# FoX attention and spectral mixing on one core: the first half of the mode weights loaded one row per partition, w_ch and the first mode products moved, f loaded on the Activation queue

## The chip, the cores and the metric

The kernel runs on one core of a Trainium2 chip. The metric is the device time of one execution in microseconds. All inputs are float32 in HBM, and the output is float32 in HBM.

## The reference, cut to what matters

Two layers are computed, one after the other. The first is causal attention with a decay that comes from forget gates f; the second mixes 64 frequency modes of the sequence with one complex matrix each, and adds a channel product.

```python
# B, H, S, Dh = 8, 8, 576, 64;  D = H * Dh = 512;  64 modes
scores = q @ k^T / sqrt(Dh) + cumsum(log f)[i] - cumsum(log f)[j], causal
x = softmax(scores) @ v                        # -> x[b, s, d], d over (h, Dh)
X  = rfft(x, axis=s)[:, :64]                   # Xr, Xi
Yr = einsum('bmd,mde->bme', Xr, w_r) - einsum('bmd,mde->bme', Xi, w_i)
Yi = einsum('bmd,mde->bme', Xr, w_i) + einsum('bmd,mde->bme', Xi, w_r)
u  = x + irfft(Yr + 1j * Yi, n=576)
out = u + relu(u @ w_ch)
```

The weights w_r and w_i are [64, 512, 512] each: 134 MB in float32 together. q, k and v are 28 MB together, w_ch is 1 MB, the output 9.4 MB.

## The kernel before, in words

**Weights.** The 64 modes' weights are cut into NT = 64 tiles of 2 MB, each loaded once into a ring of NRING = 9 buffers (`wpool`) and cast to bf16 on the way. `emit_w_load(n)` (L91) issues two DMAs for a tile, one for w_r and one for w_i, through `pool_dma`, which is GpSimd's queue in program order; the profile puts all of these under L89. Tiles 0 to 31 (n < NTH) hold rows of the first half of d, four modes a tile. Tiles 32 to 63 hold the second half of d, two modes a tile with two neighbouring rows of d in each partition. In the kernel before, tiles 0 to 31 also take two neighbouring rows of d per partition, 4 KB of HBM in one piece, with w_r on the even partitions and w_i on the odd ones (L95 to L101).

**Mode products.** `emit_modes(n)` (L118) multiplies one tile: for each of its modes and each of four blocks of e there are two (first half) or four (second half) matmuls that add up in one PSUM tile `A` of pool `psM`, which has one buffer during attention; then VectorE copies or adds `A` into `Yacc` (L155, L157) or into `YT` (L161). This frees the tile's ring buffer, and `next_w()` (L640) issues the load of the next one.

**Attention.** 32 steps s, two for each pair `pr` of (d block, batch pair). A step has the score products (L505), the exponentials on ScalarE (L512), the products with v (L550) and transposes. `emit_loads` (L215) brings k, q and v of a pair on GpSimd's queue, three buffers deep; only f (L247) and the v of the first two pairs (L226) go on SP's queue. At even steps `emit_dft` (L574) takes a finished pair to 64 modes: matmuls with the basis `bas` (L593), then, for the first half of d, copies to a tile `T` (L603, L604), four matmuls with the selection matrices `sel` that spread rows over even and odd partitions (L618), and one copy to `XT` (L629). For the last block of d there is only a strided copy (L607) and a strided negation (L611).

**Order.** The step loop (L649) loads weight tiles ahead up to the ninth in the first steps; from step 9 on it calls `emit_modes` at the end of each step, 32 tiles in 24 steps. w_ch is issued at step 10, behind the loads of the tenth tile (number 9, issued in step 9) and of a pair's k, q and v. The order that instructions take on each engine is made by the framework from the order of the program's calls, and so differs from it in places; GpSimd's DMAs keep the program's order, and in the trace no more than eight of them are outstanding at a time.

**After attention.** Tiles 32 to 63 are multiplied; between the first of them lie the products of x with w_ch (`emit_xw`, L712). After the last tile come the inverse transform, the sum and the stores (L824 to L894).

Of the kernel before, what the change touches and what calls it, by code (L numbers as in the profile page):

```python
# [8 lines left out]
F32 = mybir.dt.float32  # L9
BF16 = mybir.dt.bfloat16  # L10
# [5 lines left out]
def _strided(ap: bass.AP, free_dims, offset_elems: int = 0) -> bass.AP:  # L16
    new_ap = [list(ap.ap[0])] + [list(x) for x in free_dims]
    return bass.AP(tensor=ap.tensor, offset=ap.offset + offset_elems, ap=new_ap)
# [3 lines left out]
def kernel(  # L22
# [11 lines left out]
    nc = tc.nc  # L34
# [11 lines left out]
    MG = 4  # L46
# [20 lines left out]

    ident_bf = const.tile([128, 128], BF16, name="ident_bf")
    wch = const.tile([128, NDC, D], BF16, name="wch")
    bas = const.tile([128, NSB + 1, 2, NM], BF16, name="bas")  # L70
    sel = [const.tile([128, 130], BF16, name=f"sel{r}") for r in range(2)]
    BI = const.tile([128, SP], BF16, name="BI")

    wtiles = {}
# [16 lines left out]
    def emit_w_load(n):  # L91
        dc, g = tile_of(n)
        if n < NTH:
            wb = wpool.tile([128, MG, 2 * D], BF16, tag="wb", name="wb")
            for t, src in enumerate((moe_w_r, moe_w_i)):  # L95
                pool_dma(
                    wb[t:128:2, :, :],
                    src[
                        g * MG : (g + 1) * MG, dc * 128 : (dc + 1) * 128, :
                    ].rearrange("m (p r) e -> p m (r e)", r=2),  # L100
                )  # L101
        else:
            wb = wpool.tile([128, 2, M2, 2 * D], BF16, tag="wb", name="wb")
            parts = 2 if n == NT - 1 else 1
            for h in range(parts):
                ms = slice(h * M2 // parts, (h + 1) * M2 // parts)
                for t, src in enumerate((moe_w_r, moe_w_i)):
                    pool_dma(
                        wb[:, t, ms, :],
                        src[g * M2 : (g + 1) * M2, D // 2 : D, :][ms].rearrange(  # L110
                            "m (p r) e -> p m (r e)", r=2
                        ),
                    )
        wtiles[n] = wb
# [3 lines left out]
    def emit_modes(n):  # L118
# [8 lines left out]
        else:  # L127
            A = late["psM"].tile([128, NDC, nm, 2 * B], F32, tag="A", name="A")
        if n < NTH:
            terms = [  # L130
                (lambda mi, es, r=r: wb[:, mi, r * D + es : r * D + es + 128],
                 lambda m, r=r: XT3s[dc][:, r, :, m])
                for r in (0, 1)
            ]
        else:
            terms = [
                (lambda mi, es, t=t, r=r: wb[:, t, mi, r * D + es : r * D + es + 128],
                 lambda m, c0=c0, r=r: XT3s[2 + r][:, m, c0 : c0 + 2 * B])
                for t, c0 in ((0, B), (1, 0))
                for r in (0, 1)  # L140
            ]
        for mi in range(nm):
            m = g * nm + mi
            for eb in range(NDC):
                for i, (w_of, x_of) in enumerate(terms):
                    nc.tensor.matmul(  # L146
                        A[:, eb, mi, :],
                        lhsT=w_of(mi, eb * 128),
                        rhs=x_of(m),
                        start=(i == 0),  # L150
                        stop=(i == len(terms) - 1),
                    )
# [19 lines left out]
    with ExitStack() as actx:  # L172
# [4 lines left out]
        vap = actx.enter_context(tc.tile_pool(name="vap", bufs=2))  # L177
        epl = actx.enter_context(tc.tile_pool(name="epl", bufs=1))
        nrm = actx.enter_context(tc.tile_pool(name="nrm", bufs=4))
        tpl = actx.enter_context(tc.tile_pool(name="tpl", bufs=1))  # L180
        ssb = actx.enter_context(tc.tile_pool(name="ssb", bufs=1))
        late["psM"] = actx.enter_context(
            tc.tile_pool(name="psM", bufs=1, space=bass.MemoryType.PSUM)
# [60 lines left out]
        ident_f = scratch(128, 128)  # L244
        ftf = scratch(128, S)
        ft = ftf[:BH, :]
        nc.sync.dma_start(ft[:], f.rearrange("b h s -> (b h) s"))  # L247
        emit_loads(0)
        nc.gpsimd.memset(trimask[:, :], 1.0)
        nc.gpsimd.affine_select(  # L250
# [33 lines left out]
            nc.gpsimd.iota(m_i[:], pattern=[[1, NM]], base=0, channel_multiplier=0)  # L284
        )
        nc.vector.tensor_copy(ident_f[:, :], ident_bf[:, :])
        for r, t in enumerate(sel):
            nc.vector.memset(t[:, :], 0.0)
            nc.vector.tensor_copy(
                _strided(t[:, 1:2], [[2, 64]]), _strided(ident_bf[:, r : r + 1], [[2, 64]])  # L290
            )
        for t in VTs:
            nc.vector.memset(t[:, :, S:SP], 0.0)
        for t in KTs:
# [75 lines left out]
        def emit_basis():  # L370
# [1 line left out]
            RND = 12582912.0  # L372
            TURN = 2.0 * math.pi / S * (1.0 - 2.0e-7)
            NB1 = NSB + 1
            s_f = scratch(128, NB1)
            nc.vector.tensor_copy(s_f[:], s_i[:])
            m_f = scratch(128, NM)
            nc.vector.tensor_copy(m_f[:], m_i[:])
            ang = wide[:, 0 : 2 * NB1 * NM].rearrange(
                "p (a b c) -> p a b c", a=2, b=NB1  # L380
# [25 lines left out]
            nc.scalar.activation(Zt[:, :, :, 1], ang[:, 1, :, :], ACT.Sin, scale=-TURN)  # L406
            nc.vector.memset(Zt[64:128, 4, :, :], 0.0)
            nc.vector.memset(Zt[0:64, 5, :, :], 0.0)
            nc.vector.tensor_copy(
                bas[:, :, :, :], Zt[:, :, :, :].rearrange("p s m t -> p s t m")  # L410
            )
            coef = ssb.tile([128, 1], F32, name="coef")
            nc.vector.memset(coef[:], 2.0 / S)
            nc.vector.memset(coef[0:2, :], 1.0 / S)
# [159 lines left out]
        def emit_dft(pr):  # L574
            dc, bp, _ = steps[2 * pr]
            if dc == 2:
                return
            forms = [(dc, dc * 128, 1)] if dc < 2 else [(2, 256, 2), (3, 257, 2)]
            if dc < 2:
                if bp == 0:  # L580
                    XT3s[dc] = xtpool.tile(
                        [128, 2, 2 * B, NM], BF16, tag="XT3", name=f"XT{dc}"
                    )
                T = tpl.tile([128, 3, 2, NM], BF16, tag="T", name="T")
            for b in (2 * bp, 2 * bp + 1):
                for c, d0, st in forms:
                    if b == 0 and dc == 3:
                        XT3s[c] = xtpool.tile(
                            [128, NM, 3 * B], BF16, tag="XT3", name=f"XT{c}"
                        )  # L590
                    px = psT.tile([128, 2, NM], F32, tag="tr", name="px")
                    for sb in range(NSB):
                        nc.tensor.matmul(  # L593
                            px[:, :, :],
                            lhsT=_strided(
                                x_all[:, bp, xi(b, sb), d0 : d0 + 1], [[st, 128]]
                            ),
                            rhs=bas[:, sb if sb < 4 else 4 + b % 2, :, :],
                            start=(sb == 0),
                            stop=(sb == NSB - 1),  # L600
                        )
                    if dc < 2:
                        nc.vector.tensor_copy(T[:, 1:3, b % 2, :], px[:, :, :])  # L603
                        nc.scalar.mul(T[:, 0, b % 2, :], px[:, 1, :], -1.0)  # L604
                        continue
                    XT3 = XT3s[c]
                    nc.vector.tensor_copy(  # L607
                        _strided(XT3[:, 0, B + b : B + b + 1], [[B, 2], [3 * B, NM]]),
                        px[:, :, :],
                    )  # L610
                    nc.scalar.mul(  # L611
                        _strided(XT3[:, 0, b : b + 1], [[3 * B, NM]]), px[:, 1, :], -1.0
                    )
            if dc < 2:
                px2 = psT.tile([128, 2, 4 * NM], F32, tag="tr", name="px2")
                for r in (0, 1):
                    for t in (0, 1):
                        nc.tensor.matmul(  # L618
                            px2[:, r, :],
                            lhsT=sel[r][:, 1 - t : 129 - t],  # L620
                            rhs=T[:, 1 - t : 3 - t, :, :].rearrange(
                                "p c b m -> p (c b m)"
                            ),
                            start=(t == 0),
                            stop=(t == 1),
                            skip_group_check=True,
                        )
                XT = XT3s[dc]
                nc.vector.tensor_copy(  # L629
                    _strided(  # L630
                        XT[:, 0, 2 * bp, 0:1], [[2 * B * NM, 2], [B * NM, 2], [1, 2 * NM]]
                    ),
                    px2[:, :, :].rearrange("p r (c n) -> p r c n", c=2),
                )

        NS = len(steps)
        nload = 2
# [2 lines left out]
        def next_w():  # L640
            nonlocal nload
            if nload < NDC * NG:
                emit_w_load(nload)
                nload += 1
# [4 lines left out]
        for s in range(NS + 1):  # L649
# [2 lines left out]
                emit_loads(pr + STG - 1)  # L652
            if s < 10 and nload < min(NRING, 3 + 3 * s // 4):
                next_w()
            if s == 10:
                pool_dma(wch[:], moe_w_ch.rearrange("(eb p) e -> p eb e", p=128))
            if pr + 1 < NPR:
                emit_transposes(pr + 1, ("kq", "v")[h])
# [4 lines left out]
            if s < NS:  # L663
                emit_scores(s, 1)
                emit_scores(s, 2)
            if s >= 1:
                emit_av(s - 1, [3, 4])
            if s < NS:
# [2 lines left out]
            if s >= 1:  # L671
                vaugs.pop(s - 1)
                if h == 0:
                    emit_dft(pr - 1)
            if s > B:
                while nmode < (s - B) * NTH // (NS - B):
                    emit_modes(nmode)
                    nmode += 1
                    next_w()

    with ExitStack() as bctx:
        bsb = bctx.enter_context(tc.tile_pool(name="bsb", bufs=1))
# [255 lines left out]
```

## Time and profile before

| | us |
|---|---|
| median of 4 runs | 448.65 |
| lowest and highest | 447.41, 451.7 |
| the profiled execution | 447.73 |
| its span | 446.0 |
| TensorE busy | 335.0 |
| VectorE busy | 240.8 |
| ScalarE busy | 198.1 |
| GpSimd busy | 138.8 |

The profiled execution's own time is 1.73 us above its span. The mean granted TensorE clock is 0.806. The DMA engines moved 97.27 MB as counted at the destination, where most weights are bf16; HBM was read for 163.73 MB. A packet of a first-half weight tile is 4096 B in HBM and 2048 B in SBUF; one of w_ch is 2048 B and 1024 B.

A GB/s in a view counts bytes at the destination, so a stretch with only weights shows half of what is read. POOL is GpSimd, and a row of POOL at L89 is the issuing of one DMA, not its transfer. DMA share can be above 1, since packets of one engine overlap.

### The profile page before, as it was taken

What the parts mean: (1) busy time and instruction counts of PE and PEld (TensorE: products, weight loads), DVE (VectorE), ACT (ScalarE), POOL (GpSimd) and SP (SyncE); (2) the same over time, 40 slices, a digit from 0 to 9 for tenths busy, and PEclk for the clock granted to TensorE, in tenths of its full rate; (3) what the DMA queues carried; (4) which work ended last, traced back from release to release, by engine and by line L of the source; (5) the groups of instructions that cost most, each with busy time, mean ns of one, the idle gap of its engine ahead of it and who ended that gap; (6) DMA issues with size and microseconds to landing.
All of it is one profiled execution on the core that took longest, in us unless ns stands there. A gap on an engine that the chain in (4) does not pass through costs nothing.

```text
span 446.0 us, 11215 instructions
## 1 busy us (share of the span) xinstructions
PE 335.0 (75%) x4823; PEld 231.2 (52%) x4823; DVE 240.8 (54%) x614; ACT 198.1 (44%) x296; POOL 138.8 (31%) x194
## 2 busy tenths in 40 slices
PE   2388888999897987877877886999973247437993
PEld 1255656687665665656655665566662124323431
DVE  6768988868466555654566675233320002103893
ACT  3378877777343536436547281434320002102442
POOL 6333330532332323323323231132333232200661
PEclk9999999999766656658769595999985559756998
DMA  8999999699999999999999999999999999991697
GB/s 204 210 236 238 237 237 236 104 234 211 237 237 210 237 214 233 236 214 233 237 214 233 211 211 211 211 211 211 211 211 212 211 211 211 212 190 26 223 377 282
DMA packets 50048, 97.27 MB, mean 218 GB/s; under 512 B 3376, under 2 KB 12080, under 8 KB 50000
## 3 DMA queue, kind: packets, MB, share of 16 engines
q0 software_dynamic: 46096, 85.34, 98.1%
q1 hardware_dynamic: 3824, 11.09, 6.9%
q8 instruction: 38, 0.62, 0.5%
q10 hardware_dynamic: 80, 0.13, 0.1%
q14 instruction: 10, 0.08, 0.0%
HBM read 163.73 MB, written 9.44 MB: 388 GB/s over the span
## 4 chain that ended last, share of the span: by engine, by line
PE 40%; DMA 24%; ACT 13%; DVE 11%; issue 4%; SPq 1%; POOL 1%; DVEq 0%; ACTq 0%; POOLq 0%
DMA wb<-in_moe_w_i_dram 20%; ACT E L512 9%; PE pav L550 7%; PE A L146 6%; PE ps L505 6%; PE tp L453 6%; PE pxw L729 5%; DMA stv<-in_v_dram 3%; DVE QTs L468 2%; ACT KT L466 2%; PE vp L477 2%; PE px L593 2%; PE ptr L718 2%; DVE E L527 1%; DVE XT L607 1%
## 5 line engine op out<-in xcount | busy, mean ns | idle before, releaser
L512 ACT ACTIVATE E<-ps 128x1024 bf16<-128x1024 f32 (+1 forms) x128 | 101.7, 851 | 21.4 <-PE ps L505 14.9
L146 PE MATMUL A<-XT,wb 128*128 128x16 bf16 x2048 | 71.7, 182 | 47.3 <-DMA wb<-in_moe_w_i_dram 26.1
L146 PEld LDWEIGHTS <-wb 128*128 128x128 bf16 x2048 | 64.4, 101 | 58.5 <-DMA wb<-in_moe_w_i_dram 28.3
L89 POOL DMA_DIRECT2D wb<-in_moe_w_r_dram x65 | 43.7, 672 | 150.8 <-PE A L146 57.1
L505 PE MATMUL ps<-QTs,KT 64*128 64x64 bf16 (+4 forms) x384 | 57.0, 317 | 18.2 <-ACT E L512 17.5
L89 POOL DMA_DIRECT2D wb<-in_moe_w_i_dram x65 | 43.3, 667 | 66.7 <-DMA wb<-in_moe_w_r_dram 32.3
L550 PE MATMUL pav<-va,E 128*128 128x65 bf16 (+1 forms) x1088 | 54.5, 209 | 3.2 <-DVE va L483 1.5
L550 PEld LDWEIGHTS <-E 128*128 128x128 bf16 (+1 forms) x1088 | 45.1, 114 | 17.7 <-issue 10.0
L527 DVE TENSOR_TENSOR E<-E,trimask 128x256 bf16<-128x256 bf16 (+2 forms) x128 | 36.9, 302 | 20.4 <-ACT E L512 20.2
L161 DVE TENSOR_TENSOR YT<-A,Yacc 128x128 bf16<-128x128 f32 x24 | 8.9, 369 | 68.5 <-PE A L146 68.5
L470 ACT COPY VT<-tp 128x640 bf16<-128x640 bf16 (+1 forms) x32 | 23.3, 760 | 31.6 <-PE tp L453 31.5
L505 PEld LDWEIGHTS <-KT 64*128 64x128 bf16 x384 | 18.7, 98 | 29.9 <-issue 21.2
L466 ACT COPY KT<-tp 128x640 bf16<-128x640 bf16 (+1 forms) x32 | 21.9, 742 | 26.4 <-PE tp L453 26.4
L736 ACT CAST XW<-pxw 128x512 bf16<-128x512 f32 x36 | 20.3, 587 | 29.9 <-PE pxw L729 29.9
L729 PE MATMUL pxw<-wch,yy 128*128 128x512 bf16 x144 | 33.6, 383 | 0.0
L468 DVE COPY QTs<-tp 128x640 bf16<-128x640 bf16 (+1 forms) x32 | 23.2, 767 | 13.4 <-PE tp L453 13.2
L572 DVE TENSOR_TENSOR x_all<-pav,rcp 128x384 bf16<-128x384 f32 x64 | 29.0, 454 | 0.8
L748 ACT CAST yy<-pyw 128x512 bf16<-128x512 f32 x8 | 4.7, 586 | 51.9 <-PE pyw L741 51.9
L877 POOL TENSOR_TENSOR uo<-uo 128x1024 f32<-128x1024 f32 x7 | 16.5, 2359 | 29.9 <-DVE uo L870 26.2
L441 DVE TENSOR_TENSOR vb<-stv,wdec 128x1152 bf16<-128x1152 f32 x16 | 21.6, 1351 | 3.9 <-PE tp L453 3.9
L561 DVE RECIPROCAL rcp<-pav 128x6 f32<-128x6 f32 x64 | 12.1, 189 | 21.3 <-PE pav L550 20.5
L729 PEld LDWEIGHTS <-yy 128*128 128x128 bf16 x144 | 13.4, 99 | 16.7 <-DVE yy L723 4.4
(115 smaller groups left out, 460.7 us busy)
## 6 DMA issues: line engine op xcount, KB each, us to landing
wb<-in_moe_w_r_dram POOLq DMA_DIRECT2D x63, 512.0 KB, 16.2
wb<-in_moe_w_i_dram POOLq DMA_DIRECT2D x63, 512.0 KB, 16.5
out_dram<-uo SPq DMA_DIRECT2D x16, 512.0 KB, 3.7
stv<-in_v_dram POOLq DMA_DIRECT2D x14, 576.0 KB, 15.2
stk<-in_k_dram POOLq DMA_DIRECT2D x16, 288.0 KB, 15.2
stq<-in_q_dram POOLq DMA_DIRECT2D x16, 288.0 KB, 15.2
stv<-in_v_dram SPq DMA_DIRECT2D x2, 576.0 KB, 7.3
out_dram<-uo SPq DMA_DIRECT2D x7, 128.0 KB, 4.0
```

Source lines behind the costliest of these rows:

```text
L89: tc.keep_in_program_order(nc.gpsimd.dma_start(dst, src))
L146: nc.tensor.matmul(A[:, eb, mi, :], lhsT=w_of(mi, eb * 128), rhs=x_of(m), start=(i == 0), stop=(i == len(terms) - 1),)
L453: nc.tensor.transpose(tp[:, r - r0, :, :].rearrange("c h p -> c (h p)"), sb[:, r, :, :].rearrange("p b d -> p (b d)"), ident_bf[:, :],)
L466: nc.scalar.copy(rows(KTs[pr % 2][:, :, 0:S]), tv)
L468: nc.vector.tensor_copy(rows(QT[pr][:, :, :]), tv)
L470: nc.scalar.copy(rows(VTs[pr % 2][:, :, 0:S]), tv)
L505: nc.tensor.matmul(ps[:, b, o : o + n], lhsT=KTs[pr % 2][bs, h, jb * 128 : (jb + 1) * 128], rhs=QT[pr][bs, h, jb * 128 + c0 : jb * 128 + c ...
L512: nc.scalar.activation(E[:, :, piece * 512 : piece * 512 + w], ps[:, :, 0:w], ACT.Exp, scale=scale,)
L527: nc.vector.tensor_tensor(dg, dg, tr, ALU.mult)
L550: nc.tensor.matmul(pav[64 * half : 64 * half + w, slot, :], lhsT=E[:, b, c : c + (w - 1) * st + 1 : st], rhs=va[:, jb, b, :], start=(n == ...
L572: nc.vector.tensor_tensor(xo, pi, ri, ALU.mult)
L729: nc.tensor.matmul(pxw[:, :], lhsT=xT[:, eb, i * 128 : (i + 1) * 128], rhs=wch[:, eb, :], start=(eb == 0), stop=(eb == NDC - 1),)
```

## The change

- Tiles 0 to 31 are loaded with one row of d per partition: `wb` is [128, 2, MG, D], w_r and w_i beside each other in the free dimension, each piece 2 KB in HBM. There are two DMAs per tile, as before.
- `emit_dft` takes the first half of d the way it takes the last block: a strided copy and a strided negation straight into `XT3`. `T`, `sel`, their fill, the four matmuls of L618 and the copy of L629 go away. `bas` and the PSUM tile `px` have real and imaginary parts innermost, so the strided copy runs over (mode, part) and no longer over (part, mode).
- `emit_modes` and the loads that follow it are called in the middle of the step, ahead of the second part of the products with v, and no longer at its end.
- w_ch is issued at step 9, ahead of the tenth weight tile.
- f is issued on the Activation queue; the v of the first two pairs stays on SP.
- `s_f` and `m_f` move to a buffer of their own.

```diff
         if n < NTH:
-            wb = wpool.tile([128, MG, 2 * D], BF16, tag="wb", name="wb")
+            wb = wpool.tile([128, 2, MG, D], BF16, tag="wb", name="wb")
             for t, src in enumerate((moe_w_r, moe_w_i)):
                 pool_dma(
-                    wb[t:128:2, :, :],
+                    wb[:, t, :, :],
                     src[
                         g * MG : (g + 1) * MG, dc * 128 : (dc + 1) * 128, :
-                    ].rearrange("m (p r) e -> p m (r e)", r=2),
+                    ].rearrange("m p e -> p m e"),
                 )
...
-            terms = [
-                (lambda mi, es, r=r: wb[:, mi, r * D + es : r * D + es + 128],
-                 lambda m, r=r: XT3s[dc][:, r, :, m])
-                for r in (0, 1)
-            ]
+            terms = [(XT3s[dc], 0, t, c0) for t, c0 in ((0, B), (1, 0))]
...
-        nc.sync.dma_start(ft[:], f.rearrange("b h s -> (b h) s"))
+        nc.scalar.dma_start(ft[:], f.rearrange("b h s -> (b h) s"))
...
-                    if dc < 2:
-                        nc.vector.tensor_copy(T[:, 1:3, b % 2, :], px[:, :, :])
-                        nc.scalar.mul(T[:, 0, b % 2, :], px[:, 1, :], -1.0)
-                        continue
                     XT3 = XT3s[c]
                     nc.vector.tensor_copy(
-                        _strided(XT3[:, 0, B + b : B + b + 1], [[B, 2], [3 * B, NM]]),
+                        _strided(XT3[:, 0, B + b : B + b + 1], [[3 * B, NM], [B, 2]]),
                         px[:, :, :],
                     )
-                    nc.scalar.mul(
-                        _strided(XT3[:, 0, b : b + 1], [[3 * B, NM]]), px[:, 1, :], -1.0
-                    )
-            if dc < 2:
-                px2 = psT.tile([128, 2, 4 * NM], F32, tag="tr", name="px2")
-                for r in (0, 1):
-                    for t in (0, 1):
-                        nc.tensor.matmul(
-                            px2[:, r, :],
...
+                    nc.scalar.mul(XT3[:, :, b : b + 1], px[:, :, 1:2], -1.0)
...
-            if s == 10:
+            if s == 9:
                 pool_dma(wch[:], moe_w_ch.rearrange("(eb p) e -> p eb e", p=128))
...
                 emit_scores(s, 1)
                 emit_scores(s, 2)
+            if s > B:
+                while nmode < (s - B) * NTH // (NS - B):
+                    emit_modes(nmode)
+                    nmode += 1
+                    next_w()
             if s >= 1:
                 emit_av(s - 1, [3, 4])
...
                 if h == 0:
                     emit_dft(pr - 1)
-            if s > B:
-                while nmode < (s - B) * NTH // (NS - B):
-                    emit_modes(nmode)
-                    nmode += 1
-                    next_w()
```

More of the change, by code (lines that the diff above doesn't have):

```diff
@@ L69 @@
     wch = const.tile([128, NDC, D], BF16, name="wch")
-    bas = const.tile([128, NSB + 1, 2, NM], BF16, name="bas")
-    sel = [const.tile([128, 130], BF16, name=f"sel{r}") for r in range(2)]
+    bas = const.tile([128, NSB + 1, NM, 2], BF16, name="bas")
     BI = const.tile([128, SP], BF16, name="BI")
@@ L129, in emit_modes @@
         if n < NTH:
-            terms = [
-                (lambda mi, es, r=r: wb[:, mi, r * D + es : r * D + es + 128],
-                 lambda m, r=r: XT3s[dc][:, r, :, m])
-                for r in (0, 1)
-            ]
+            terms = [(XT3s[dc], 0, t, c0) for t, c0 in ((0, B), (1, 0))]
         else:
             terms = [
[L137 to L140, printed above, removed]
+                (XT3s[2 + r], r, t, c0) for t, c0 in ((0, B), (1, 0)) for r in (0, 1)
             ]
@@ L144, in emit_modes @@
             for eb in range(NDC):
-                for i, (w_of, x_of) in enumerate(terms):
+                for i, (XT3, r, t, c0) in enumerate(terms):
                     nc.tensor.matmul(
                         A[:, eb, mi, :],
-                        lhsT=w_of(mi, eb * 128),
-                        rhs=x_of(m),
+                        lhsT=wb[:, t, mi, r * D + eb * 128 : r * D + (eb + 1) * 128],
+                        rhs=XT3[:, m, c0 : c0 + 2 * B],
                         start=(i == 0),
@@ L179 @@
         nrm = actx.enter_context(tc.tile_pool(name="nrm", bufs=4))
-        tpl = actx.enter_context(tc.tile_pool(name="tpl", bufs=1))
         ssb = actx.enter_context(tc.tile_pool(name="ssb", bufs=1))
@@ L286 @@
         nc.vector.tensor_copy(ident_f[:, :], ident_bf[:, :])
[L287 to L290, printed above, removed]
-            )
         for t in VTs:
@@ L374, in emit_basis @@
             NB1 = NSB + 1
-            s_f = scratch(128, NB1)
+            s_f = ssb.tile([128, NB1], F32, name="s_f")
             nc.vector.tensor_copy(s_f[:], s_i[:])
-            m_f = scratch(128, NM)
+            m_f = ssb.tile([128, NM], F32, name="m_f")
             nc.vector.tensor_copy(m_f[:], m_i[:])
@@ L408, in emit_basis @@
             nc.vector.memset(Zt[0:64, 5, :, :], 0.0)
-            nc.vector.tensor_copy(
-                bas[:, :, :, :], Zt[:, :, :, :].rearrange("p s m t -> p s t m")
-            )
+            nc.vector.tensor_copy(bas[:, :, :, :], Zt[:, :, :, :])
             coef = ssb.tile([128, 1], F32, name="coef")
@@ L578, in emit_dft @@
             forms = [(dc, dc * 128, 1)] if dc < 2 else [(2, 256, 2), (3, 257, 2)]
-            if dc < 2:
[L580 to L584, printed above, removed]
             for b in (2 * bp, 2 * bp + 1):
                 for c, d0, st in forms:
-                    if b == 0 and dc == 3:
+                    if b == 0:
                         XT3s[c] = xtpool.tile(
@@ L590, in emit_dft @@
                         )
-                    px = psT.tile([128, 2, NM], F32, tag="tr", name="px")
+                    px = psT.tile([128, NM, 2], F32, tag="tr", name="px")
                     for sb in range(NSB):
@@ L601, in emit_dft @@
                         )
-                    if dc < 2:
-                        nc.vector.tensor_copy(T[:, 1:3, b % 2, :], px[:, :, :])
-                        nc.scalar.mul(T[:, 0, b % 2, :], px[:, 1, :], -1.0)
-                        continue
                     XT3 = XT3s[c]
                     nc.vector.tensor_copy(
-                        _strided(XT3[:, 0, B + b : B + b + 1], [[B, 2], [3 * B, NM]]),
+                        _strided(XT3[:, 0, B + b : B + b + 1], [[3 * B, NM], [B, 2]]),
                         px[:, :, :],
                     )
-                    nc.scalar.mul(
-                        _strided(XT3[:, 0, b : b + 1], [[3 * B, NM]]), px[:, 1, :], -1.0
-                    )
-            if dc < 2:
-                px2 = psT.tile([128, 2, 4 * NM], F32, tag="tr", name="px2")
-                for r in (0, 1):
-                    for t in (0, 1):
-                        nc.tensor.matmul(
-                            px2[:, r, :],
[L620 to L634, printed above, removed]
+                    nc.scalar.mul(XT3[:, :, b : b + 1], px[:, :, 1:2], -1.0)
         NS = len(steps)
```

## The prediction

> **What bounds the kernel now.** I read the page's slices first, for the resource that is never idle, then the windows around the one stretch where it is, then GpSimd's timeline for the cause.
>
> ```profile
> DMA  8999999699999999999999999999999999991697
> GB/s 204 210 236 238 237 237 236 104 234 211 237 237 210 237 214 233 236 214 233 237 214 233 211 211 211 211 211 211 211 211 212 211 211 211 212 190 26 223 377 282
> ...
> PE 40%; DMA 24%; ACT 13%; DVE 11%; issue 4%; SPq 1%; POOL 1%; DVEq 0%; ACTq 0%; POOLq 0%
> ```
>
> The DMA row is full in slices 1 to 34, but for slice 7 (78 to 89 us). The 211 GB/s are bytes at the destination; weights are read as float32, so 422 GB/s leave HBM. The chain of waits puts 40% on TensorE, but it follows a queue that is never empty: GpSimd issues a load when a ring buffer comes free, and that load then stands behind others. So the end is the end of the DMA stream, about 404 us, plus a tail of some 41 us that the change doesn't touch. No engine is above 75%. A saving on an engine counts only where the stream runs dry.
>
> The windows show the dry place, w_ch's transfer and a stretch of 4 KB pieces. The two figures after the engines' columns are DMA share and GB/s, behind the granted clock:
>
> ```profile
> 79.70:83.70 4.00, 4.00 (x85) 3.19 (x84) 3.03 (x11) 3.23 (x6) 1.42 (x3) 1.00 0.02 6
> 94.80:95.80 1.00, 1.00 (x38) 1.00 (x36) 0.14 (x2) 1.00 (x1) 1.00 (x2) 1.00 1.24 207
> 320.00:380.00 60.00, 31.55 (x662) 22.75 (x660) 10.05 (x28) 6.58 (x12) 18.59 (x26) 0.69 1.12 211
> ```
>
> For 4 us nothing moves. GpSimd's timeline says why:
>
> ```profile
> 63.59 0.62 POOL L89 DMA_DIRECT2D wb<-in_moe_w_i_dram  x1 [1.81 <-DMA wb<-in_moe_w_r_dram]
> 82.28 0.81 POOL L89 DMA_DIRECT2D wb<-in_moe_w_r_dram  x1 [18.07 <-PE A L146]
> ...
> 85.82 0.80 POOL L89 DMA_DIRECT2D wch<-in_moe_w_ch_dram  x1
> ```
>
> All nine ring buffers are filled; the tenth tile waits 18.07 us for the first mode products, and k, q, v of a pair and w_ch stand behind it in the same queue. The last packet before starts at 79.65 us and the next at 83.78: a gap of 4.13 us.
>
> **The change part by part.**
>
> *The gap.* w_ch now comes ahead of the tenth tile, waits for no ring buffer, and follows the ninth tile. Its 512 pieces of 2 KB take 512 / 200 = 2.56 us (200 packets started per us, counted in the packet records at 94.4 to 96.0 us). 4.13 - 2.56 leaves 1.57 us. The nine tiles before come 9 x 0.12 = 1.1 us later (next part), and the first products are called ahead of the second av part, the step's last score piece and the v transposes; in the trace these take about 2 us before the products' start at 80.81 us. More than 1.57 us is covered, so I take the whole gap: **-4.1 us**; at least w_ch's own 2.6 us. What follows stays fed: from 83.3 us on the tenth tile (5.1), a pair's k, q, v (4.3) and the eleventh (5.1) last to 97.8 us, and the third mode tile freed its buffer by 94.7 us already.
>
> *First-half pieces of 2 KB for 4 KB.* A tile is 1024 packets for 512. From 320 to 380 us 6143 packets of 4 KB start, 102.4 per us, so a tile takes 5.00 us. At w_ch's 200 per us it takes 1024 / 200 = 5.12 us, 2.4% more; w_ch has the same shape of destination, 128 partitions with four pieces of 1 KB. 32 tiles x 0.12 = **+3.8 us**. The GB/s of the windows, 207 against 211, is a second reading, 1.9% or 3.0 us. From below: the window 94.70 to 96.00, which keeps some bytes of a v load, reads 211, no loss. From above: the records give one 2 KB packet 98.1 ns and one 4 KB packet 173.6 ns, and 2 x 98.1 is 13% more, 0.65 us a tile, +20.9 us. I take starts per us, since packets of an engine overlap (share 1.12) and their durations are no price. GpSimd issues w_ch in 0.80 us for 0.62 of a weight DMA; with two per 5 us and several queued, nobody waits for that.
>
> The Trainium skill speaks against any price here: "DMA: Bandwidth & Descriptors", section Specifications, gives 512 B as the smallest transfer at line rate, so that 2 KB would cost nothing and the sum would be -4.4 us. The same page, section Why small descriptors are slow (HBM only), has about three fixed cycles a packet beside one per 32 B; by that, an estimate, 2 x (64 + 3) stand against 128 + 3, 2.3%, and the sum would be -0.7 us. The measured 2.4% decides for the second.
>
> *f on the Activation queue.* On SP f takes 0.59 us (0.81 to 1.40) before v's two issues; v now starts 0.6 us sooner, while in 2 to 4 us the stream stands at 226 GB/s counted at float32 and isn't full. I take half, **-0.3 us**, between 0 and -0.6. If f's issue stands behind the 1.28 us table load of ScalarE at 0.80 us, the cumulative sums start 1.3 us later; the stream doesn't wait for them, and the first products, late by that, still fall in the 1.57 us that are covered twice.
>
> *The frequency step.* Per pair of the first half:
>
> ```profile
> L618 PE MATMUL px<-T,sel x32: 272/278/418, 44.8 to 147.3; 128*128 128x256 bf16 x32
> L603 DVE CAST T<-px x16: 279/281/292, 43.9 to 144.9; 128x128 bf16<-128x128 f32 x16
> L604 ACT ACTIVATE T<-px x16: 224/224/255, 44.3 to 145.2; 128x64 bf16<-128x64 f32 x16
> L607 DVE CAST XT<-px x16: 735/748/984, 234.2 to 275.0; 128x128 bf16<-128x128 f32 x16
> L611 ACT ACTIVATE XT<-px x16: 452/464/474, 235.0 to 275.8; 128x64 bf16<-128x64 f32 x16
> L629 DVE CAST XT<-px x8: 690/692/693, 45.4 to 147.8; 128x512 bf16<-128x512 f32 x8
> ```
>
> TensorE loses 32 x 0.278 = 8.9 us. VectorE pays 16 x (0.748 - 0.281) = 7.5 and saves 8 x 0.692 = 5.5; the new order of the copy isn't in the trace, so it lies between 0.281 and 0.748 us, and I take the latter. ScalarE pays 16 x (0.464 - 0.224) = 3.8 us. Over 120 us of attention that is 1 us a pair at most in either direction, and the stream covers it: **0**. `sel`'s fill at the start, under 1 us of VectorE, and the new place of `s_f` and `m_f` are 0 for the same reason.
>
> *Mode products in mid-step.* The same products, loads and copies in another order, nothing added. What waits behind them on TensorE is the second av part, a score piece and the v transposes, and with these ScalarE's next exponential. `psM` has one buffer, so a second tile in a step waits for VectorE's copy, 0.51 or 0.52 us each time before (117.72, 119.36, 210.41 us). How much slack hides it is read where the queue is thinnest:
>
> ```profile
> 296.63 0.72 POOL L89 DMA_DIRECT2D wb<-in_moe_w_r_dram  x1 [4.91 <-PE A L146]
> ```
>
> Issued bytes less moved bytes, at 421 GB/s read, leave 3.8 us of queue there; first data follow 0.7 us after an issue ends (83.09 to 83.78). So attention, which ends at 276 us, may end **3.0 us** later before the stream runs dry. Price 0 within that.
>
> **Sum:** -4.1 + 3.8 - 0.3 = -0.6 us. The profiled execution (447.73 us: span 446.0 and 1.73 around it) becomes 447.1. It is 0.9 us under the median of the runs shown; on that median, 448.65, the forecast is **448.0 us**. A measurement of this kernel tells about 1%, 4.5 us, from no change, so this is no change. The case's own range is 447.0 (3.0 us for the pieces by the windows, gap and start at their best: -4.1 + 3.0 - 0.6 = -1.7) to 451.0 (against the fastest stretch of 4 KB pieces, 103.1 starts per us from 13.5 to 21.5 us, 0.15 us a tile or 4.9 us, and only w_ch's part of the gap: 4.9 - 2.6 = +2.3).
>
> **Rivals.**
>
> 1. *Short pieces cost more in bulk than w_ch shows.* w_ch is one transfer of 2.6 us, with a step of 256 KB between a partition's pieces where the weights have 1 MB, and 32 tiles in a row may fall between starts and durations. With the durations' price the sum is 20.9 - 4.4 = +16.5, **465 us**; half of that price gives 454.7. It decides from 82.5 ns a packet and engine (80 for w_ch): 32 x 32 x 8.7 ns a pair = 8.9 us, which with the -4.4 is 1% slower. For it: durations, and w_ch's landing at 11.9 us tells nothing of a long run. Against: 2304 B pieces of k and q also go at about 400 GB/s read in their dense stretches. Chance 0.20.
>
> 2. *TensorE's order becomes the bound.* Should each of the 24 steps from step 9 on lengthen by one 0.5 us wait on `psM`, attention ends 12 us later; 3.0 are covered, so the end moves by 9 us, **457.7 us**. Against: the removed 8.9 us of TensorE work and the engine order, which already interleaves products with scores. It decides when attention ends after 279 us. Chance 0.08.
>
> 3. *The change doesn't close the gap*, beyond w_ch: products start as late as before. Then -2.6 + 3.8 - 0.3 = +0.9, **449.5 us**, within 1%. Chance 0.07.
>
> 4. *Short pieces cost nothing*: -4.1 - 0.3 = -4.4, **444.2 us**, at the edge of faster. Windows that read 211 for both speak for it, packet starts against. Chance 0.10.
>
> The forecast itself has 0.55. Faster by over 1% needs the fourth case with a little more: 0.08. Slower by over 1% takes the first and second, 0.26 of their 0.28; the rest, 0.66, is within 1%. The range leaves out about a tenth at each side: 444.5 to 457.
>
> **What the changed profile would show.** Slice 7 of the DMA row full, no stretch without packets from 20 to 404 us; w_ch issued about 64 to 70 us, the tenth tile's wait shorter than 18 us. GB/s of pure first-half stretches about 206 (rival 1: under 200). The last weights landing within 2 us of where they land now, and the tail 41 us long. Attention over before 279 us. A stream that stands still after 276 us would show the second rival right; a last landing later than 409 us with a full DMA row, the first.

## The result, and the profile after

The changed kernel takes 447.18 us (median) against 447.55 us for the kernel before, measured over many runs of both; the ratio is 0.9981 with a 95% interval of 0.9972 to 0.999. The forecast was 0.6 us less than before; 0.4 us less was measured. As a time it was 448.0 us, since it stood on the median of four runs, 448.65 us, which is 1.1 us above that of the many. The two profiled executions are 446.39 us (changed, span 444.7) and 447.73 us (before, span 446.0), further apart than the medians; the point on the tail below says where that lies.

The page of the changed kernel, in the rows that the prediction read in the page of the kernel before:

```profile
DMA  9999999999999999999999999999999999991698
GB/s 203 206 233 233 234 233 234 177 234 206 234 233 208 233 227 213 234 218 223 233 211 232 212 211 212 211 211 211 211 211 211 211 211 211 211 198 25 224 353 314
...
DMA 52%; PE 29%; DVE 7%; issue 2%; ACT 2%; POOL 1%; SPq 1%; DVEq 0%; POOLq 0%; ACTq 0%
```

Slice 7 of the DMA row is full now, at 177 GB/s where 104 stood. The other full slices of the first half are a few GB/s lower than before (233 or 234 for 236 to 238): the shorter pieces. The chain of waits now names DMA for 52%, where before it followed TensorE.

Windows of the changed kernel; the last two columns are again DMA share and GB/s:

```profile
82.00:85.00 3.00, 3.00 (x55) 2.25 (x55) 2.40 (x6) 2.20 (x4) 2.59 (x4) 1.00 0.78 115
79.70:83.70 4.00, 3.77 (x79) 2.92 (x79) 3.25 (x12) 2.84 (x8) 1.48 (x2) 1.00 0.90 152
320.00:380.00 60.00, 26.81 (x597) 19.86 (x596) 8.40 (x23) 4.10 (x7) 17.18 (x24) 0.63 1.12 211
```

The 4 us that carried 6 GB/s carry 152. The stretch of 4 KB pieces from 320 to 380 us is as it was. But from 82 to 85 us the stream is thin, 115 GB/s. A stretch that holds only first-half weights in both kernels, first the kernel before, then the changed one, shows the shorter pieces alone, 212 and 206 GB/s:

```profile
38.00:45.00 7.00, 5.84 (x94) 3.99 (x93) 6.57 (x22) 5.94 (x10) 1.74 (x3) 1.00 1.12 212
```

```profile
38.00:45.00 7.00, 5.95 (x92) 3.87 (x88) 6.16 (x19) 6.22 (x9) 2.20 (x3) 1.00 1.24 206
```

GpSimd's timeline of the changed kernel:

```profile
67.08 0.74 POOL L88 DMA_DIRECT2D wch<-in_moe_w_ch_dram  x1 [1.75 <-DMA wb<-in_moe_w_i_dram]
82.08 0.74 POOL L88 DMA_DIRECT2D wb<-in_moe_w_r_dram  x1 [14.26 <-PE A L138]
```

w_ch goes out behind the ninth tile, as foreseen. The tenth tile is issued at 82.08 us, hardly sooner than before (82.28).

To follow the stream over the whole kernel I used the packet records, as in the prediction: each kind of packet has an interval between starts on one engine in full stretches of this kind (156.2 ns for 4 KB of HBM, 80.1 for 2 KB, 41.8 for 1 KB, 89.8 for the 2304 B of k and q, and by a fit over all full stretches 175.4 for the 4608 B of v). What a stretch's length exceeds the sum of these intervals, divided by 16 engines, is lost: time in which the stream stands still or runs thin, called a hole here. "Stream end" is the start of the last weight packet. The median is over all runs, the other columns are from the one profiled execution of each kernel. All in us:

| kernel | median | stream end | lost 78 to 84 | lost 84 to 110 | lost 276 to 314 |
|---|---|---|---|---|---|
| before | 447.55 | 403.4 | 5.1 | 0.8 | 0.0 |
| changed | 447.18 | 403.4 | 1.2 | 0.5 | 0.0 |
| e1_wch9 | 445.46 | 401.6 | 2.5 | 0.5 | 1.5 |
| e2_rows4k | 447.29 | 403.0 | 2.9 | 2.0 | 1.5 |
| e3_wch10 | 449.98 | 406.0 | 3.9 | 0.4 | 0.1 |
| e4_f_sync | 445.72 | 401.8 | 0.2 | 0.0 | 0.0 |
| e6_end_step | 448.76 | 404.7 | 1.5 | 1.9 | 0.1 |
| e7_full_4k | 443.52 | 398.6 | 0.0 | 0.7 | 0.5 |
| e8_full_2k | 445.78 | 402.1 | 0.0 | 0.0 | 0.1 |
| e5_rows1k | 454.72 | 411.0 | 0.0 | 1.4 | 0.0 |

Over the whole stream the kernel before has 391.3 us of packets and loses 12.1; the changed kernel has 395.4 and loses 7.9. So 4.1 us of dearer packets stand against 4.2 us of filled holes, and the stream ends at the same time.

### The profile page after: what moved, and what is told of

Its sections match the earlier page's. It is cut to its first block, busy times and chain, and to the rows that moved or that the text cites. A ratio compares the mean times of both kernels' runs of the same rounds, so it can differ in the third digit from the quotient of the medians.

```text
span 444.7 us, 11099 instructions
## 1 busy us (share of the span) xinstructions
PE 333.9 (75%) x4791; PEld 225.2 (51%) x4791; DVE 235.8 (53%) x602; ACT 202.1 (45%) x296; POOL 146.7 (33%) x194
## 4 chain that ended last, share of the span: by engine, by line
DMA 52%; PE 29%; DVE 7%; issue 2%; ACT 2%; POOL 1%; SPq 1%; DVEq 0%; POOLq 0%; ACTq 0%
DMA wb<-in_moe_w_i_dram 24%; DMA stk<-in_k_dram 11%; DMA stq<-in_q_dram 8%; PE pxw L680 6%; PE ps L489 4%; PE pav L534 4%; PE tp L437 4%; PE A L138 4%; DMA stv<-in_v_dram 4%; DMA wb<-in_moe_w_r_dram 3%; PE px L571 2%; DVE XT L581 2%; PE ptr L669 2%; PE vp L461 1%; DVE uo L821 1%
## 5 line engine op out<-in xcount | busy, mean ns | idle before, releaser
L496 ACT ACTIVATE E<-ps 128x1024 bf16<-128x1024 f32 (+1 forms) x128 | 104.3, 858 | 35.5 <-PE ps L489 24.3
L138 PE MATMUL A<-XT,wb 128*128 128x16 bf16 x2048 | 69.9, 172 | 49.0 <-DMA wb<-in_moe_w_i_dram 29.3
L88 POOL DMA_DIRECT2D wb<-in_moe_w_r_dram x65 | 47.5, 731 | 144.6 <-PE A L138 43.7
L88 POOL DMA_DIRECT2D wb<-in_moe_w_i_dram x65 | 47.3, 727 | 67.3 <-DMA wb<-in_moe_w_i_dram 36.9
L489 PE MATMUL ps<-QTs,KT 64*128 64x64 bf16 (+4 forms) x384 | 63.4, 324 | 6.2 <-ACT E L496 6.1
L534 PE MATMUL pav<-va,E 128*128 128x65 bf16 (+1 forms) x1088 | 56.5, 213 | 2.8 <-DVE x_all L556 1.2
L534 PEld LDWEIGHTS <-E 128*128 128x128 bf16 (+1 forms) x1088 | 46.6, 117 | 13.8 <-issue 6.6
L511 DVE TENSOR_TENSOR E<-E,trimask 128x256 bf16<-128x256 bf16 (+2 forms) x128 | 38.9, 311 | 6.0 <-ACT E L496 5.3
L437 PE MATMUL tp<-ident_bf,kb 128*128 128x128 bf16 x144 | 16.9, 270 | 19.9 <-DVE kb L421 18.7
L581 DVE CAST XT<-px 128x128 bf16<-128x128 f32 x32 | 20.9, 805 | 8.8 <-PE px L571 8.6
```

The source lines that it names most:

```text
L88: tc.keep_in_program_order(nc.gpsimd.dma_start(dst, src))
L138: nc.tensor.matmul(A[:, eb, mi, :], lhsT=wb[:, t, mi, r * D + eb * 128 : r * D + (eb + 1) * 128], rhs=XT3[:, m, c0 : c0 + 2 * B], start=(i ...
L437: nc.tensor.transpose(tp[:, r - r0, :, :].rearrange("c h p -> c (h p)"), sb[:, r, :, :].rearrange("p b d -> p (b d)"), ident_bf[:, :],)
L489: nc.tensor.matmul(ps[:, b, o : o + n], lhsT=KTs[pr % 2][bs, h, jb * 128 : (jb + 1) * 128], rhs=QT[pr][bs, h, jb * 128 + c0 : jb * 128 + c ...
L496: nc.scalar.activation(E[:, :, piece * 512 : piece * 512 + w], ps[:, :, 0:w], ACT.Exp, scale=scale,)
L511: nc.vector.tensor_tensor(dg, dg, tr, ALU.mult)
```

## The experiments

The theory (A) is that of the prediction: the DMA stream sets the end, holes in it cost their length, and a packet costs a fixed part besides its bytes. The rivals: the engines set the end and the hole lies beside them (B), short pieces cost nothing (C), and those named at each run. Each run's ratio is to the kernel before, measured beside it.

### e1_wch9: w_ch alone

```diff
 # kernel before
-            if s == 10:
+            if s == 9:
                 pool_dma(wch[:], ...)
```

> The kernel before with one edit, w_ch issued at step 9 ahead of the tenth weight tile. Theory A (the DMA stream sets the end, and what fills its dry stretch comes off the time): w_ch's 2.56 us move into the 4.13 us gap, which shrinks to about 1.5 us; time 447.55 - 2.6 = 445.0 us. Theory B (the engines' chain sets the end, the gap is beside it): no change, 447.5 us.

445.46 us, ratio to before 0.9963 (0.9941 to 0.9985). The hole shrinks by 2.6 us, as w_ch's length says, and the stream ends 1.8 us sooner, not 2.6: 1.5 us are lost in 276 to 314 us, where before lost nothing. Theory B is out. The late loss is the second rival's limit met from the other side. After attention the loads are issued when they were before (296.63 us at the thinnest place):

```profile
296.53 0.72 POOL L89 DMA_DIRECT2D wb<-in_moe_w_r_dram  x1 [4.91 <-PE A L146]
```

A stream that comes sooner uses up the slack there as well as an attention that ends later. The prediction found 3.0 us of it. This stream comes 2.9 us sooner (the losses from 78 to 110 us fall from 5.9 to 3.0) and loses 1.5, so the slack was about 1.4 us, by this account.

### e3_wch10: the change without w_ch's move

```diff
 # changed kernel
-            if s == 9:
+            if s == 10:
                 pool_dma(wch[:], ...)
```

> The changed kernel with w_ch issued at step 10 again. Theory A: w_ch's 2.56 us no longer lie in the dry stretch before the tenth tile, 449.8 us. Theory B (or: the later products and slower tiles had closed the gap without w_ch): 447.2 us.

449.98 us, ratio to before 1.0053 (1.0038 to 1.0068), 2.8 us above the changed kernel. The loss at 78 to 84 us goes from 1.2 to 3.9. So w_ch's move closes two thirds of what is left of the gap without it, and without it the change is a loss.

### e4_f_sync: f back on SP

```diff
 # changed kernel
-        nc.scalar.dma_start(ft[:], f.rearrange("b h s -> (b h) s"))
+        nc.sync.dma_start(ft[:], f.rearrange("b h s -> (b h) s"))
```

> The changed kernel with f back on SP ahead of v. Theory A: f lands 2.4 us sooner, so attention and the first mode products start some 2 us sooner, and the 1.2 us that the stream still loses between 78 and 84 us go: 446.0 us. Theory D (v's earlier start on SP is worth its 0.3 us and the later products cost nothing): 447.5 us.

445.72 us, ratio to before 0.9959 (0.9946 to 0.9972): 1.5 us better than the changed kernel. ScalarE's timeline shows what f did. First the changed kernel, where f is issued on ScalarE's queue (ACTq):

```profile
0.81 0.55 ACTq L238 DMA_DIRECT2D Yacc<-in_f_dram  x1
...
6.05 0.68 ACT L285 ACTIVATE Yacc<-Yacc 64x576 f32<-64x576 f32 x1 [3.38 <-DMA Yacc<-in_f_dram]
```

then this run, whose only difference is f's queue, and the kernel before:

```profile
3.65 0.68 ACT L285 ACTIVATE Yacc<-Yacc 64x576 f32<-64x576 f32 x1 [1.56 <-DMA Yacc<-in_f_dram]
```

```profile
3.68 0.68 ACT L299 ACTIVATE Yacc<-Yacc 64x576 f32<-64x576 f32 x1 [1.59 <-DMA Yacc<-in_f_dram]
```

Issued at the same 0.81 us, f arrives 2.4 us later beside v than ahead of it: in the packet records of the changed kernel v's packets start at 1.9 us and f's at 3.8, so f goes behind v's first part. The first copy of k (`kb`) is at 21.48 us for 19.68 in this run and 19.52 before, and the first mode products inherit that. The bulk of the first tile's products starts late in the changed kernel, 2.3 us sooner in this run:

```profile
80.86 0.92 PE L138 MATMUL A<-XT,wb 128*128 128x16 bf16 x31
```

```profile
78.54 0.92 PE L138 MATMUL A<-XT,wb 128*128 128x16 bf16 x31
```

With f on SP the tenth tile is issued sooner too:

```profile
79.76 0.74 POOL L88 DMA_DIRECT2D wb<-in_moe_w_r_dram  x1 [12.35 <-PE A L138]
```

and the stream loses 0.2 us there in place of 1.2.

### e6_end_step: mode products at the end of the step

```diff
 # changed kernel: the block moves from behind emit_scores(s, 2) to behind emit_dft(pr - 1)
             if s > B:
                 while nmode < (s - B) * NTH // (NS - B):
                     emit_modes(nmode)
                     nmode += 1
                     next_w()
```

> The changed kernel with the mode products called at the end of the step again. Theory A: the first products come 1 to 2 us later, the stream is dry that much longer between 82 and 86 us and thinner to 110 us: 448.5 us. Theory F (the calls' place means nothing to the stream, since the framework interleaves): 447.2 us.

448.76 us, ratio to before 1.0023 (1.0013 to 1.0034), 1.6 us above the changed kernel. The tenth tile is issued at 83.19 us, 1.1 later, and the stream loses 1.9 us for 0.5 between 84 and 110. So the place of the calls counts, although the framework interleaves (theory F is out).

### e2_rows4k: the change without its short pieces

```diff
 # kernel before, 4 KB pieces and selection matmuls kept
-        nc.sync.dma_start(ft[:], ...)
+        nc.scalar.dma_start(ft[:], ...)
-            if s == 10:
+            if s == 9:
...  # and the block of mode products behind emit_scores(s, 2)
```

> The whole change but for the weight rows: first-half tiles keep 4 KB pieces and the selection matmuls; w_ch, mode products and f as changed. Theory A (2 KB pieces cost 0.15 us a tile, 198.6 starts per us against 102.2 for 4 KB): 32 x 0.15 = 4.8 us come off the changed kernel's 447.2, but the ninth tile lands 1.3 us sooner, so that 1.3 us more of the stream are dry before the tenth: 443.7 us. Theory C (2 KB pieces cost nothing): 447.2 us. If packet durations were the price, 20 us would come off, 427 us.

447.29 us, ratio to before 0.9995 (0.997 to 1.002): a miss, 3.6 us over what theory A gave, and just what C gave. `s_f` and `m_f` stay as before in this run too. The windows say which of the two it is:

```profile
82.40:85.00 2.60, 2.60 (x52) 1.87 (x50) 2.40 (x7) 1.98 (x4) 1.20 (x2) 1.00 0.02 6
285.00:296.00 11.00, 10.68 (x130) 6.68 (x131) 3.68 (x10) 4.75 (x9) 2.85 (x4) 1.00 1.10 195
...
320.00:380.00 60.00, 33.52 (x671) 24.27 (x674) 10.46 (x28) 7.97 (x14) 18.57 (x26) 0.69 1.12 211
```

The shorter stream is there (packets worth 391 us), but its gain is lost again: a hole of 2.8 us before the tenth tile, now issued at 83.80 us, a thin stretch to 110 us (2.0), and one after attention, 195 GB/s for 211 (1.5). These are some 4.5 us more than the changed kernel loses in the same three stretches. In my expectation only the first was counted, and at 1.3 us. It also took 4.8 us as the price of the pieces, from 198.6 starts per us; the full stretches give 199.7, and a price of 4.1. f is on the Activation queue here as well: the first copy of k is at 21.63 us, for 19.21 in e1_wch9, and the first mode products at 82.33 us for 80.50. So f's lateness can account for most of what this run has lost against e1_wch9 (445.46 us); this kernel with f on SP was not run. This left the price of the pieces to be shown in a stream without holes.

### e7_full_4k and e8_full_2k: both piece sizes without holes

```diff
 # e7: kernel before; e8: changed kernel with f on SP
-            if h == 0 and pr + STG - 1 < NPR:
+            if s != 10 and h == 0 and pr + STG - 1 < NPR:
                 emit_loads(pr + STG - 1)
...
+            if s == 9:
+                emit_loads(pr + STG)
                 pool_dma(wch[:], ...)
...
-                if nmode % 4 and nx < B:
+                if nmode > NTH + 4 and nmode % 4 and nx < B:
                     emit_xw(nx)
```

> The kernel before, its 4 KB pieces kept, with the stream's two thin places filled: at step 9 k, q and v of the eighth pair and w_ch are issued ahead of the tenth weight tile, and after attention five tiles are multiplied before the first products of x with w_ch, so that ring buffers come free sooner. Theory A (the stream is the end): of the 12.3 us that the stream of before loses, 5.1 at 78 to 84 us go, the late thinning (1.5 us in the run with w_ch alone moved) does not appear; 447.5 - 5 = 442.5 us. Theory E (engines after attention are the end as soon as the stream is faster than before): not under 445 us.

> The same two fillings in the changed kernel, f on SP: 2 KB pieces in a stream that is never dry. Theory A: 445.7 us as the changed kernel with f on SP, since that one loses nothing there; so 2 KB pieces cost 445.7 - 442.5 = 3 to 4.5 us against the same kernel with 4 KB pieces. Theory C (pieces cost nothing, the 4 KB run was slow from its matmuls): as fast as the 4 KB kernel with fillings.

e7 takes 443.52 us, ratio to before 0.9904 (0.9888 to 0.9921), and is the fastest of all, though 1.0 us over theory A's 442.5; e8 takes 445.78 us, ratio 0.9956 (0.9942 to 0.997). Theory E fell. The window of e7 that held the hole before (34 GB/s there):

```profile
78.00:84.00 6.00, 6.00 (x109) 4.54 (x109) 4.67 (x15) 4.35 (x6) 1.42 (x2) 1.00 1.16 258
```

e8 is no faster than e4_f_sync (445.72), which had no hole left to fill. Between e7 and e8 the stream ends differ by 3.5 us, within the 3 to 4.5 expected, but the medians by 2.3, which is less. The two also differ in the frequency step and in the place of the mode products; the account of the stream separates that from the pieces: 391.3 and 395.4 us of packets, 7.3 and 6.7 us lost. So short pieces have a price, theory C is out, and e2's lack of gain came from its holes. The 1.2 us between the two differences lie behind the issue of the last store: the span ends 6.3 us after it in e7 and 5.1 in e8. Some 0.7 of that is the store's landing, told at the end.

### e5_rows1k: pieces of 1 KB

```diff
 # changed kernel, tiles 0 to 31
-            wb = wpool.tile([128, 2, MG, D], BF16, tag="wb", name="wb")
+            wb = wpool.tile([128, 2, 2, MG, D // 2], BF16, tag="wb", name="wb")
...
-                    ].rearrange("m p e -> p m e"),
+                    ].rearrange("m p (x e) -> p x m e", x=2),
```

> The changed kernel with 1 KB pieces in tiles 0 to 31, 2048 packets a tile. Theory A (a packet costs 4.2 ns an engine besides its bytes, from 156.2 ns for 4 KB and 80.2 for 2 KB): 42.2 ns a packet, 168.8 a 4 KB worth for 160.4, so 32 x 32 x 8.4 ns = 8.6 us more, less 1.2 us of thin stream that is covered: 454.6 us. Theory C (pieces cost nothing at 1 KB too): 447.2 us; if the cost grows faster than per packet, over 460 us.

454.72 us, ratio to before 1.0154 (1.0131 to 1.0176); theory A had 454.6. The parts of that sum were not met so well: the packets grew by 7.2 us for the 8.6 expected, and the losses, which were to fall by 1.2 us, grew by 0.5. In full stretches packets of 1 KB start at 382.6 per us, 41.8 ns an engine. With 80.1 for 2 KB and 156.2 for 4 KB a straight line goes through the three: 0.0372 ns a byte and 3.7 ns a packet give 41.8, 79.9 and 156.1. The 2304 B of k and q lie near it too (89.4 by the line, 89.8 measured). The Trainium skill, "DMA: Bandwidth & Descriptors", section Why small descriptors are slow (HBM only), tells of about three fixed cycles a packet beside one per 32 B, which at this slope is 3.6 ns, an estimate; the 3.7 of the runs agree with it. The same page's Specifications give 512 B as enough for line rate; here 1 KB pieces are 7.0% slower than 4 KB ones (4 x 41.8 against 156.2), and the measurement decides.

## Why the prediction was right, point by point

- **The bound.** Right. In the profiled executions the time lies 43.0 to 44.8 us behind the stream's end in all ten kernels, while that end moves over 12.4 us. Five kernels that filled or opened holes (e1, e3, e4, e6, e7) moved with it, in both directions.
- **The gap, -4.1 us.** Right in size: the losses from 78 to 110 us fell from 5.9 to 1.7. Wrong in one part of its reason: "the first products ... about 2 us before" did not come. Before, they start here:

```profile
80.81 1.17 PE L146 MATMUL A<-XT,wb 128*128 128x16 bf16 x32
```

  In the changed kernel one matmul starts at 79.92 us and the bulk at 80.86, because attention started 2 us later with f. With f on SP (e4_f_sync) the earlier place does bring them 2.3 us forward, and then the losses fall to 0.2. So the gap and the thin stretch behind it were worth 5.7 us, not 4.1, and f took 1.5 of them back. In the changed kernel w_ch (2.6 us) and the later arrival of the slower tiles (some 1.1 us) covered the rest, all but a thin 1.2 us.
- **2 KB pieces, +3.8 us.** Right in mechanism and nearly in size. In full stretches 102.4 and 199.7 starts per us make 5.00 and 5.13 us a tile, or 4.1 us for 32 tiles; the packets of the two whole streams differ by 4.1 too. w_ch's 1.6 us, with 200 starts per us, were a short sample, but a good one. Packet durations (98 and 174 ns) would have been a price of 20.9 us, and were rightly not taken.
- **f on the Activation queue, -0.3 us.** The step that failed, in sign: v's packets start sooner (the first at 1.9 us; before, f's 64 packets start at 2.2 and v's follow them), but the stream's loss over the first 20 us stays (3.2 and 3.3 us), and f's late landing costs 1.5 us by e4_f_sync. The prediction looked for the delay in the table load, which came behind f's issue (1.39 us) and did no harm; it didn't ask what f shares the DMA engines with. That a late start is hidden, "covered twice", was wrong too, as the first products used that cover up.
- **The frequency step, 0.** Right for this change. The copy takes 728 ns, near the 748 taken:

```profile
L581 DVE CAST XT<-px x32: 709/728/957, 45.9 to 268.6; 128x128 bf16<-128x128 f32 x32
L585 ACT ACTIVATE XT<-px x32: 458/464/658, 46.6 to 269.3; 128x64 bf16<-128x64 f32 x32
```

  But attention now ends at about 270 us, 6 us sooner, and TensorE waits for k, as the changed kernel's waits from 100 to 280 us say:

```profile
PE tp L437 <- DVE kb L421: 17.8, 5, 5.3
```

  The last negation of the frequency step (L585 above) starts at 275.8 us before, at 277.7 in e2_rows4k, which keeps the selection matmuls, at 272.2 in e6_end_step, which doesn't but has the products at the step's end, and at 269.3 in the changed kernel. So most of the gain goes with the removed step, and 2.9 us with the products' place. The slack matters: e4's stream ends nearly as early as e1's and loses nothing after attention, where e1, with attention ending as before, loses 1.5 us.
- **Mode products in mid-step, 0.** The place is worth 1.6 us (e6_end_step). In the prediction it stood only as help for the gap; its effect on the loads to 110 us was missed. The 3.0 us of slack after attention were too many: e1 shows about 1.4.
- **The rivals.** The first (pieces dearer in bulk) fell: 32 tiles in a row cost what w_ch's starts said, within 0.3 us. The second did not come in the changed kernel; its limit showed in e1, from a stream that was sooner, and in e2, where attention ended 1.9 us later as well. The third's condition came true, as the products started as late as before, but not its 449.5 us: it left out the 1.1 us that the slower tiles cover and the thin stretch to 110 us. The fourth fell with e5, and with the full stretches of 2 KB.
- **The signs.** The DMA row is full; w_ch is issued at 67.08 us; the tenth tile's wait is 14.26 us for 18.07; pure first-half stretches show 206 GB/s; the last weights start at the same time as before.
- **The tail, "some 41 us that the change doesn't touch".** The last product starts at 403.94 us before and 403.88 after, the last store is issued at 440.16 and 439.66, and the span ends 5.8 and 5.0 us behind that. So of the 1.3 us between the spans 0.06 is stream and the rest tail. The medians are only 0.4 us apart, and the changed kernel's profiled execution is 0.8 us faster than its median: part of this difference is one execution's chance.
- That the sum came out is partly luck. The holes gave 5.7 us where 4.1 were forecast, and f cost 1.5 where 0.3 was to be gained; the two errors, 1.6 and 1.8 us, cancel.

## What to carry to other kernels

When a transfer stream is busy from one end to the other, make an account of it: packets times their interval in a full stretch of one kind, and the holes. Each edit is then worth what it does to packets or holes, and a gain in one place can be lost at the next thin place, as with 4 KB pieces here (nothing at 447.29 us, 2.3 us once the holes were filled). Put loads that wait for nothing ahead of the one that waits for a buffer, and put a small transfer that starts a chain ahead of the big one, not beside it.

## What the runs showed of the hardware that was not expected

A 144 KB load issued on a second queue at the same time as two of 576 KB landed 2.4 us later than the same load issued 0.65 us ahead of them on one queue (used at 6.05 us in the changed kernel, at 3.65 in e4_f_sync).

The last store, 128 KB on the Activation queue, lands later in the kernels with 4 KB pieces. The DMA issues of the kernel before, and of the changed one:

```profile
out_dram<-uo ACTq DMA_DIRECT2D x1, 128.0 KB, 4.7
```

```profile
out_dram<-uo ACTq DMA_DIRECT2D x1, 128.0 KB, 3.9
```

It is 4.4 to 4.8 us in the four kernels with 4 KB pieces (before, e1, e2, e7) and 3.8 to 4.1 us in the six with shorter ones, though no weight moves then. What causes it was not tried, and is open.
